# Turning x with VectorE blocks and SBUF-to-SBUF transfers in place of TensorE transposes, under a replanned order

## The chip, the cores and the metric

The kernel runs on one core of one Trainium2 chip. The core has a matrix engine (TensorE, PE in the profile, with its weight loads as PEld), VectorE (DVE), ScalarE (ACT), GpSimd (POOL) and SyncE (SP), each working through a queue of its own in order, and 16 DMA engines. A step on one engine waits for steps on others by semaphores. The metric is the time of one execution on the device in microseconds (us), lower is better.

## What is computed

All in float32. The inputs are q, k, v of shape (8 batches, 8 heads, 576 positions, 64), g_norm (64), and three weights that arrive as float64: w_val and w_out (512 x 512) and conv_w (5 x 512). The reference, cut to what matters:

```python
kv  = einsum('bhsd,bhse->bhde', k, v)
out = einsum('bhsd,bhde->bhse', q, kv)
out = out / sqrt(mean(out * out, axis=-1) + 1e-6) * g_norm
x   = out.transpose(0, 2, 1, 3).reshape(B, S, H * D)        # (8, 576, 512)
gate_pre[:, s] = sum over k of conv_w[k] * xp[:, k + s]     # xp: x with 4 rows of zeros ahead
gate = 1 / (1 + exp(-gate_pre))
result = (gate * (x @ w_val)) @ w_out
```

## The kernel before, in words

Work is cut by batch. For each of the 8 batches there is an attention part and a gated part.

**Attention.** `kv_product` (matmuls at L330) makes the 64 x 64 product of k and v for each head, `kv_copy` (L340) puts pairs of heads on the diagonal of a 128 x 128 tile. q has to be turned so that its 64 features lie on partitions: for batches 0 and 1 by TensorE (`turn_q_rows`, L360, and ScalarE copies that sort the columns), for batches 2 to 7 (`TURNED = 2`) by one VectorE block transpose for each pair of heads (`turn_q`, L348). Then the 576 positions are taken in five chunks, four of 128 and a tail of 64, tail first and the others downwards (`ORDER`). For each chunk: `raw_product` (L399, four matmuls into one of two PSUM banks), `square` on ScalarE (L413), `sums` on VectorE (L421), `powers` on GpSimd (L427, the inverse root), `normalise` on VectorE (L434), which writes the chunk's x as rows of positions, `turn_x` (L445), which turns each 128 x 128 block of x with a TensorE transpose against an identity matrix into PSUM, and `keep_x` on ScalarE (L452), which copies it to SBUF and multiplies by the column gcol (g_norm times 8). What stands in `xT` then is x with features on partitions and positions along the free axis, in the order "t within n", position = t x 18 + n, with n counting 18 blocks of 32 columns. In this order the shift by one position of the convolution is a shift by one block of 32 columns; four extra blocks in front (the halo) are filled by four GpSimd copies (`halo`, L460).

**Gated part.** `gate_start` (L464, ScalarE) makes the first tap of the convolution for one group of 128 features, four `gate_tap` (L470, VectorE, 128 x 576 each) add the others, `gate_end` (L477, ScalarE) applies the sigmoid. `val_product` (L482) is x times w_val, eight products of four matmuls a batch (the profile counts eight matmuls for four of the code, the transposes of x once); `gated` (L491, VectorE) multiplies by the gate. `out_product` (L501) is the product with w_out, 4 or 5 chunks a batch, `keep_out` (L509) copies it out of PSUM, `store` (L516) issues four DMAs of 64 KB on SP's queue.

**Weights** are staged as raw 64-bit words (`stage`, L247) and narrowed to float32 in eight steps a tile, five on VectorE and three on ScalarE (L267 to L293).

**Order.** Nothing is ordered by the loops. Each step is added to a `Planner` with its engine, a modelled duration, a wanted time (`want`), what it needs, gives, takes from a ring of buffers and frees. The planner walks through modelled time: a step can start once its needs are there, a buffer of its ring is free, and not more than `ahead` us before its want (0 for loads); among those that can start first, the one with the earlier want goes. This gives each engine's fixed queue order, which is then emitted. The rings that bear on the change: x rows 3, xT 3, gate 5, qT 2, the raw banks 2, staged weights 3 (4 buffers exist). DMAs are issued by SP alone, except two small loads of g_norm from ScalarE.

Of the kernel before, what the change touches and what calls it, by code (L numbers as in the profile page):

```python
# [15 lines left out]
P = 128  # L16
EPS = 1e-6


class Planner:  # L20


# [5 lines left out]
    HOP = 0.15  # L28
    LANDING = 1.9

    def __init__(self, rings):
        self.rings = {name: {"size": n, "taken": [], "freed": {}} for name, n in rings.items()}
        self.steps, self.done, self.pending = [], {}, []

    def add(self, engine, time, want, fn, *args, needs=(), gives=(), takes=(), frees=(), load=0.0, ahead=12.0):
        self.steps.append(dict(
            engine=engine, time=time, want=want, fn=fn, args=args, needs=list(needs),
            gives=list(gives), takes=list(takes), frees=list(frees), load=load, ahead=ahead, at=len(self.steps)))

    def ready(self, step):  # L40

        t = step["want"] - step["ahead"]
        for key in step["needs"]:
# [4 lines left out]
        for name, _ in step["takes"]:  # L48
# [41 lines left out]
def kernel(  # L90
# [26 lines left out]

    nc = tc.nc  # L120
    B, H, S, D = q.shape
    C = H * D
# [24 lines left out]
    def ps(kind, shape, name):  # L147
        return psum.tile(shape, FP32, tag=kind, bufs=BANKS[kind], name=name)

    plan = Planner({  # L150
# [3 lines left out]
    })  # L154


    tails = [[const.tile([P, H, D], FP32, name=f"{n}l{i}") for n in ("k", "v")] for i in range(2)]
# [84 lines left out]
    def stage(key, src, n, m):  # L242

        size = src.shape[-1]
        t = loads.tile([P, C, 2], U32, tag="w64", bufs=4, name=f"w64_{key[0]}{key[1]}")
        t = t[0:n, 0:m * size, :]
        nc.sync.dma_start(  # L247
            out=t.rearrange("p (m c) w -> p m (c w)", m=m), in_=src.bitcast(U32))
        staged[key] = t

    def narrow(key, dst, n):


        w = staged[key]
        rows, size = w.shape[0], w.shape[1]
        split = lambda a: a if len(dst.shape) == 2 else a.rearrange(
            "p (m c) -> p m c", m=dst.shape[1])
        lo, hi = w[:, :, 0], w[:, :, 1]
        if n == 0:
            staged[key, "parts"] = [  # L260
                work.tile([P, C], kind, tag=tag, bufs=bufs, name=f"{tag}_{key[0]}{key[1]}")[
                    0:rows, 0:size]
                for tag, kind, bufs in (("wexp", U32, 2), ("wman", U32, 1), ("wmf", FP32, 1))]
        e, m, mf = staged[key, "parts"]

        if n == 0:
            nc.vector.tensor_scalar(  # L267
                out=e, in0=hi, scalar1=20, scalar2=0x7FF,
                op0=ALU.logical_shift_right, op1=ALU.bitwise_and,
            )  # L270
        elif n == 1:
            nc.scalar.activation(out=e, in_=e, func=AF.Relu, bias=biases[0:rows, 0:1])
        elif n == 2:
            nc.scalar.activation(out=e, in_=e, func=AF.Relu, bias=biases[0:rows, 1:2], scale=-1.0)
        elif n == 3:
            nc.scalar.activation(
                out=e, in_=e, func=AF.Identity, bias=biases[0:rows, 2:3], scale=-float(1 << 23))
        elif n == 4:
            nc.vector.scalar_tensor_tensor(
                out=e, in0=hi, scalar=0x80000000, in1=e, op0=ALU.bitwise_and, op1=ALU.bitwise_or,  # L280
            )
        elif n == 5:

            nc.vector.tensor_scalar(
                out=m, in0=hi, scalar1=0xFFFFF, scalar2=1 << 20,
                op0=ALU.bitwise_and, op1=ALU.bitwise_or,
            )
        elif n == 6:
            nc.vector.scalar_tensor_tensor(  # L289
                out=mf, in0=lo, scalar=2.0 ** -32, in1=m, op0=ALU.mult, op1=ALU.add,  # L290
            )
        else:
            nc.vector.scalar_tensor_tensor(  # L293
                out=dst, in0=split(mf), scalar=2.0 ** -20, in1=split(e.bitcast(FP32)),
                op0=ALU.mult, op1=ALU.mult,
            )

# [19 lines left out]
    def keep_cw():  # L317

        nc.vector.tensor_scalar_mul(gcol[:], gcol[:], math.sqrt(D))
        nc.vector.tensor_copy(cwT[:], st["cwps"][:])  # L320

    def kv_product(b, hp):
        if hp == 0:
# [21 lines left out]
        return st["qT", b]  # L345

    def turn_q(b, hp):
        nc.vector.transpose(out=new_qT(b)[:, hp, :], in_=st["q", b, hp][:, :, 0:TB])  # L348

    def size(c):  # L350
        return P if c < NJ else T
# [78 lines left out]

    def normalise(b, c):
        n = heads(c)
        x = work.tile([P, C], FP32, tag="x", bufs=3, name=f"x{b}_{c}")
        nc.vector.tensor_tensor(  # L434
            out=x[:, 0:n * D].rearrange("p (h e) -> p h e", h=n),
            in0=st["raw", b, c][:, 0:n * D].rearrange("p (h e) -> p h e", h=n),
# [11 lines left out]
    def keep_x(b, c):  # L448
# [2 lines left out]
        px = st["px", b, c][:].rearrange("p k t -> p (k t)")[:, 0:NK * m]  # L451
        nc.scalar.activation(  # L452
            out=xTs[b % 3][:, :, first:first + m], in_=px.rearrange("p (k t) -> p k t", k=NK),
            func=AF.Copy, scale=gcol[:],
        )

    def halo(b):
        for kc in range(NK):
# [1 line left out]
            nc.gpsimd.tensor_copy(row[:, 0:K - 1, 1:TB], row[:, NB:NB + K - 1, 0:TB - 1])  # L460

    def gate_start(b, jt):
        gate = work.tile([P, S], FP32, tag="gate", bufs=5, name=f"gate{b}_{jt}")
        nc.scalar.activation(  # L464
            out=gate[:], in_=xTs[b % 3][:, jt, HALO:SX], func=AF.Copy, scale=cwT[:, K - 1, jt:jt + 1])
        st["gate", b, jt] = gate
# [62 lines left out]
    def attention(b, first, step, kv_first, turn_first):  # L529

        slow = 1.7 if b == 0 else 1.0
        for hp in range(HP):
# [8 lines left out]
            )  # L541
            if b >= TURNED:
                plan.add(
                    "DVE", 0.77, turn_first + 1.5 * hp, turn_q, b, hp,
                    needs=[("q", b, hp)] + after("qT", b, hp - 1), gives=[("qT", b, hp)],
                    takes=[("qT", b)] if hp == 0 else [], frees=[("q", (b, hp))],
                )
# [23 lines left out]
        for n, c in enumerate(ORDER):  # L571
# [35 lines left out]
            if n == 1:  # L607
                plan.add(
                    "POOL", 1.2, t + 7.0, halo, b, needs=[("xT", b, NJ), ("xT", b, NJ - 1)],
                    gives=[("halo", b)],  # L610
                )

    def gates(b, first, step):
        for jt in range(NK):
# [91 lines left out]
    def weight(key, want, first, step):  # L706
# [5 lines left out]
        for n in range(8):  # L712
# [1 line left out]
            plan.add(  # L714
                "ACT" if n in (1, 2, 3) else "DVE", (0.45, 0.75, 0.75, 0.75, 0.7, 0.45, 0.7, 0.7)[n] * small,
                first + n * step, narrow_weight, *key, n,
                needs=[("staged", key) if n == 0 else ("narrow", key, n - 1)],
                gives=[("narrow", key, n)] + ([key] if n == 7 else []),
                takes=[(ring, key)] if ring else [],
                frees={6: [("w64", key), ("wman", key)], 7: [("wexp", key), ("wmf", key)]}.get(n, []),  # L720
# [67 lines left out]
```

## Time and profile before

| | |
|---|---|
| median of 3 runs | 367.56 us (366.39 to 369.91) |
| profiled execution | 370.04 us |
| its span, first to last instruction | 368.2 us |
| mean granted TensorE clock | 0.979 |
| HBM read, written | 39.21 MB, 9.44 MB |

The profile is of one execution. The span is shorter than the time of the execution by what lies before the first instruction and after the last. "Busy" leaves out DMA issues, semaphores and branches. "Idle before" is the time an engine stood still just ahead of a group, with what ended that wait. The chain is followed back from the last instruction to whatever released it, so its shares add up to the span, while busy times of engines that work side by side do not. Matmuls are pipelined: a single one's duration (275 ns for a transpose of x) overlaps its neighbours', and the chain or a window says better what a group takes.

### The profile page before, as it was taken

Reading aid. Unit: us, or ns where it says so; the run is one execution under the profiler, and the core shown is the slowest. Engines: PE = TensorE matmul, PEld = TensorE weight load, DVE = VectorE, ACT = ScalarE, POOL = GpSimd, SP = SyncE. Lnnn points to the kernel's source line nnn. Section 1 sums busy time; section 2 is a strip of 40 time slices with the busy share of each in tenths; the row PEclk is TensorE's granted clock in tenths of the full one; section 3 lists DMA queues with packets and bytes.
Section 4 is the critical chain, followed back from the end, with each engine's and each line's share of the span. In section 5 each row is a group of like instructions: output and inputs, shape, how many; then the busy total and the mean of one; then the engine's idle time right before and its main releaser. Section 6 shows DMA issues by size and latency. Waiting matters only on the chain.

```text
span 368.2 us, 5537 instructions
## 1 busy us (share of the span) xinstructions
PE 341.9 (93%) x2065; PEld 232.0 (63%) x2065; DVE 215.7 (59%) x363; ACT 142.4 (39%) x253; POOL 73.9 (20%) x82
## 2 busy tenths in 40 slices
PE   4677899869799999999999999999999999999994
PEld 3676687648564786477646785578546874674441
DVE  3075999979932995957329764956239645920000
ACT  3385766715344335422333425313253335201111
POOL 2045025200431153003410241005300450000000
PEclk9989999969899999999999999999999999999998
DMA  7999977922024960595029821981122002201322
GB/s 222 291 291 336 257 204 233 292 61 64 0 53 140 265 194 16 167 274 166 8 65 229 268 84 39 311 239 34 29 57 59 2 0 53 63 2 29 86 75 67
DMA packets 42936, 49.01 MB, mean 133 GB/s; under 512 B 14218, under 2 KB 34718, under 8 KB 42910
## 3 DMA queue, kind: packets, MB, share of 16 engines
q1 hardware_dynamic: 42750, 48.67, 48.0%
q8 instruction: 16, 0.26, 0.3%
q14 instruction: 10, 0.08, 0.1%
q10 hardware_dynamic: 160, 0.00, 0.0%
HBM read 39.21 MB, written 9.44 MB: 132 GB/s over the span
## 4 chain that ended last, share of the span: by engine, by line
PE 83%; SPq 6%; DVE 5%; DMA 3%; ACT 2%; issue 1%; DVEq 0%; ACTq 0%
PE val L482 33%; PE out L501 33%; PE raw L399 8%; PE kv L330 4%; PE xTps L445 4%; DMA v<-in_v_dram 3%; SPq L196 2%; DVE gate L470 2%; SPq L205 2%; SPq L247 1%; PE qTps L360 1%; DVE gv L491 1%; DVE ss L421 0%; DMA out_dram<-ot 0%; DVE wmf_wout L289 0%
## 5 line engine op out<-in xcount | busy, mean ns | idle before, releaser
L482 PE MATMUL val<-xT,wval 128*128 128x288 f32 x512 | 136.4, 414 | 6.9 <-DVE gv L491 6.1
L501 PE MATMUL out<-wout,gv 128*128 128x512 f32 x288 | 127.2, 595 | 0.0
L470 DVE SCALAR_TENSOR_TENSOR gate<-xT,cwT,gate 128x576 f32<-128x576 f32 x128 | 102.8, 816 | 30.2 <-ACT gate L464 27.5
L482 PEld LDWEIGHTS val<-xT,wval 128*128 128x128 f32 x512 | 94.7, 192 | 33.5 <-DVE gv L491 7.2
L427 POOL TENSOR_TENSOR rt<-ss,mhalf 128x8 f32<-128x8 f32 (+1 forms) x40 | 63.5, 1591 | 226.5 <-DVE ss L421 226.5
L501 PEld LDWEIGHTS out<-wout,gv 128*128 128x128 f32 x288 | 53.9, 192 | 61.3 <-issue 61.0
L509 ACT COPY ot<-out 128x512 f32<-128x512 f32 x36 | 21.0, 583 | 82.7 <-PE out L501 53.4
L491 DVE TENSOR_TENSOR gv<-val,gate 128x288 f32<-128x288 f32 x64 | 28.6, 452 | 25.7 <-PE val L482 25.4
L399 PE MATMUL raw<-kvbd,qT 128*128 128x128 f32 (+1 forms) x320 | 41.5, 289 | 1.9 <-ACT kvbd L340 1.9
L399 PEld LDWEIGHTS raw<-kvbd,qT 128*128 128x128 f32 (+1 forms) x320 | 37.6, 191 | 6.9 <-issue 3.4
L452 ACT ACTIVATE xT<-xTps,gcol 128x512 f32<-128x512 f32 (+1 forms) x40 | 25.8, 645 | 39.0 <-PE xTps L445 39.0
L413 ACT ACTIVATE sq<-raw 128x512 f32<-128x512 f32 (+1 forms) x40 | 22.2, 554 | 37.4 <-PE raw L399 37.3
L434 DVE TENSOR_TENSOR x<-raw,rt 128x512 f32<-128x512 f32 (+1 forms) x40 | 25.2, 630 | 19.5 <-POOL rt L427 19.4
L477 ACT ACTIVATE gate<-gate 128x576 f32<-128x576 f32 x32 | 21.8, 682 | 36.2 <-DVE gate L470 36.2
L421 DVE TENSOR_REDUCE ss<-sq 128x8 f32<-128x520 f32 (+1 forms) x40 | 25.3, 634 | 16.3 <-ACT sq L413 16.1
L330 PE MATMUL kv<-v,k 128*64 128x64 f32 x512 | 21.3, 229 | 3.6 <-DMA v<-in_v_dram 3.6
L330 PEld LDWEIGHTS kv<-v,k 128*64 128x64 f32 x512 | 18.4, 142 | 9.8 <-issue 8.6
L445 PE MATMUL xTps<-ident,x 128*128 128x128 f32 x144 | 22.4, 275 | 2.3 <-DVE x L434 2.2
L445 PEld LDWEIGHTS xTps<-ident,x 128*128 128x128 f32 x144 | 17.7, 141 | 10.5 <-issue 6.6
L464 ACT ACTIVATE gate<-xT,cwT 128x576 f32<-128x576 f32 x32 | 22.2, 764 | 0.3
L348 DVE STREAM_TRANSPOSE qT<-q 128x576 f32<-128x576 f32 x24 | 18.1, 766 | 5.4 <-DMA q<-in_q_dram 5.4
L360 PE MATMUL qTps<-ident,q 128*64 128x128 f32 (+1 forms) x160 | 11.6, 308 | 5.1 <-DMA q<-in_q_dram 5.1
(52 smaller groups left out, 99.6 us busy)
## 6 DMA issues: line engine op xcount, KB each, us to landing
q<-in_q_dram SPq DMA_DIRECT2D x96, 140.0 KB, 4.1
out_dram<-ot SPq DMA_DIRECT2D x144, 64.0 KB, 1.7
k<-in_k_dram SPq DMA_DIRECT2D x16, 512.0 KB, 5.4
v<-in_v_dram SPq DMA_DIRECT2D x16, 512.0 KB, 6.6
q<-in_q_dram SPq DMA_DIRECT2D x4, 512.0 KB, 6.4
w_wval<-in_moe_w_val_dram SPq DMA_DIRECT2D x4, 512.0 KB, 8.6
w_wout<-in_moe_w_out_dram SPq DMA_DIRECT2D x4, 512.0 KB, 5.7
kl<-in_k_dram SPq DMA_DIRECT2D x8, 128.0 KB, 6.3
```

The lines of the kernel that those rows point to most:

```text
L330: nc.tensor.matmul(kvp[r * D:(r + 1) * D, hp, :], st["k", b, half][:, h, j, :] if j < NJ else kl[:, 2 * hp + r, :], st["v", b, half][:, h, ...
L399: nc.tensor.matmul(raw[row * m:(row + 1) * m, col * P:(col + 1) * P], st["qT", b][:, hp, c * P:c * P + m], kv_bd[b % 2][:, hp, :], start=T ...
L413: nc.scalar.activation(out=sq[:, 0:n, 0:D], in_=st["raw", b, c][:, 0:n * D].rearrange("p (h e) -> p h e", h=n), func=AF.Square,)
L421: nc.vector.reduce_sum(out=ss[:, 0:n], in_=st["sq", b, c][:, 0:n], axis=AX.X)
L427: nc.gpsimd.tensor_tensor(out=rt[:, 0:n], in0=st["ss", b, c][:, 0:n], in1=mhalf[:, 0:n], op=ALU.pow)
L434: nc.vector.tensor_tensor(out=x[:, 0:n * D].rearrange("p (h e) -> p h e", h=n), in0=st["raw", b, c][:, 0:n * D].rearrange("p (h e) -> p h ...
L445: nc.tensor.transpose(px[:, col, :], st["x", b, c][:, col * P:(col + 1) * P], ident[:])
L452: nc.scalar.activation(out=xTs[b % 3][:, :, first:first + m], in_=px.rearrange("p (k t) -> p k t", k=NK), func=AF.Copy, scale=gcol[:],)
L470: nc.vector.scalar_tensor_tensor(out=gate[:], in0=xTs[b % 3][:, jt, tap * TB:tap * TB + S], scalar=cwT[:, tap, jt:jt + 1], in1=gate[:], op ...
L482: nc.tensor.matmul(val[:], wval[:, kc, jt * P:(jt + 1) * P], xTs[b % 3][:, kc, HALO + n * SV:HALO + (n + 1) * SV], start=(kc == 0), stop=( ...
L491: nc.vector.tensor_tensor(out=gv[:, jt, first:first + SV], in0=st["val", b, jt, n][:], in1=st["gate", b, jt][:, n * SV:(n + 1) * SV], op=A ...
L501: nc.tensor.matmul(po[:], gv[:, jt, c * P:(c + 1) * P], wout[:, jt, :], start=(jt == 0), stop=(jt == NK - 1),)
```

## The change

For batches 2 to 7 the four full chunks of x are no longer turned by TensorE:

- `turn_blocks` (VectorE) transposes the 128 x 512 rows of x in blocks of 32 x 32 into a tile y, one instruction a chunk.
- `move_blocks` (GpSimd queue) then puts the blocks onto their partitions: for each of four groups of columns four DMAs from SBUF to SBUF, each 32 partitions x 4 x 512 bytes (64 KB). All four chunks must be in y before the first group. The groups go from the last columns to the first; the first of them is also given the tail's copy as a need. Per batch that makes 16 transfers.
- So that a block of 32 rows of a chunk is a block of 32 columns of xT, chunk c now holds the blocks n = c, c + 4, c + 8, c + 12 of q: `turn_q` becomes five instructions over the same 576 columns.
- The tail chunk of every batch, and all chunks of batches 0 and 1, still go through `turn_x` and `keep_x`.
- `keep_x` no longer multiplies by gcol. It is multiplied into the taps (`keep_cw`) and into w_val (the last narrowing step), for which that step of w_val now needs cwT.
- Rings: x 3 to 2, gate 5 to 4, staged weights to 3 buffers, y new with 2.
- The planner: `ahead` 12 to 40 us by default; rings tails, kvbd, xT and gv are taken strictly batch by batch; and the table `SHIFTS` is added to the wants, by step and batch (or weight tile).

```diff
+SHIFTS = {
+    "gate_start": {0: 7},
+    "gate_tap": {3: 16.5, 7: 9},
+    "gated": {0: 14.5, 6: -13.5},
+    "halo": {2: -0.5, 4: -69, 6: -5.5},
+    "kv_product": {1: -16, 6: -3},
+    "load_half": {("k", 3): -7, ("k", 4): -27, ("k", 6): -21.5, ("v", 0): -5, ("v", 1): 18, ("v", 2): -5,
+        ("v", 4): -34, ("v", 6): -74},
+    "load_q": {3: 2.5, 4: -1, 5: -3, 6: -5, 7: -12.5},
+    "load_q_rows": {0: -273, 1: 28.5},
+    "load_tails": {0: -53, 3: -20.5, 4: 24},
+    "move_blocks": {3: 35, 7: 5.5},
+    "narrow_weight": {("wout", 1): -14.5, ("wout", 2): -68},
+    "normalise": {2: -16.5},
+    "out_product": {2: -291.5},
+    "powers": {7: -166.5},
+    "raw_product": {0: -10.5},
+    "square": {1: 0.5, 5: -17.5},
+    "stage_weight": {("cw", 0): -385, ("wout", 0): -43, ("wout", 3): -18.5, ("wval", 1): -83.5,
+        ("wval", 2): -40, ("wval", 3): -31.5},
+    "store": {0: -1.5},
+    "sums": {0: -19, 2: -73.5, 4: 6},
+    "turn_q": {3: -15, 5: -59.5},
+    "turn_x": {0: -9.5},
+    "val_product": {0: 15, 1: 47.5, 2: 72, 3: 70.5, 4: 57, 5: 52},
+}
...
-    def add(self, engine, time, want, fn, *args, needs=(), gives=(), takes=(), frees=(), load=0.0, ahead=12.0):
+    def add(self, engine, time, want, fn, *args, needs=(), gives=(), takes=(), frees=(), load=0.0, ahead=40.0):
+        ints = [a for a in args if isinstance(a, int)]
+        which = tuple(a for a in args if isinstance(a, str)) + tuple(ints[:1])
+        want += SHIFTS.get(fn.__name__, {}).get(which[0] if len(which) == 1 else which, 0.0)
...
+            if name in self.by_batch and len(ring["taken"]) != owner:
+                return None
...
+                out=dst, in0=split(mf), scalar=gcol[:] if key[0] == "wval" else 2.0 ** -20, in1=split(e.bitcast(FP32)),
...
-        nc.vector.tensor_copy(cwT[:], st["cwps"][:])
+        nc.vector.tensor_scalar_mul(cwT[:], st["cwps"][:], gcol[:])
+        nc.vector.tensor_scalar_mul(gcol[:], gcol[:], 2.0 ** -20)
...
-        nc.vector.transpose(out=new_qT(b)[:, hp, :], in_=st["q", b, hp][:, :, 0:TB])
+
+        q, qT = st["q", b, hp], new_qT(b)[:, hp, :]
+        for c in range(NJ):
+            nc.vector.transpose(out=qT[:, c * P:(c + 1) * P], in_=q[:, c:NJ * HB:NJ, 0:TB])
+        nc.vector.transpose(out=qT[:, SF:S], in_=q[:, NJ * HB:NB, 0:TB])
...
-            func=AF.Copy, scale=gcol[:],
+            func=AF.Copy,
         )
+
+    def turn_blocks(b, c):
+        if ("y", b) not in st:
+            st["y", b] = work.tile([P, C // TB, NJ, TB], FP32, tag="y", name=f"y{b}")
+        nc.vector.transpose(
+            out=st["y", b][:, :, c, :], in_=st["x", b, c][:].rearrange("p (k i) -> p k i", i=TB))
+
+    def move_blocks(b, a):
+
+        y = st["y", b][:].rearrange("p (k i) c t -> p i k (c t)", i=HB)
+        first = HALO + a * P
+        for i in range(HB):
+            nc.gpsimd.dma_start(
+                out=xTs[b % 3][i * TB:(i + 1) * TB, :, first:first + P],
+                in_=y[a * TB:(a + 1) * TB, i])
...
+            if b >= TURNED and c < NJ:
+                plan.add(
+                    "DVE", 0.75, t + 5.5, turn_blocks, b, c,
+                    needs=[("x", key)] + ([("y", b, ORDER[n - 1])] if n > 1 else []),
+                    gives=[("y", b, c)], takes=[("y", b)] if n == 1 else [], frees=[("x", key)],
+                )
+                continue
...
+        t = first + 4 * step + 6.0
+        if b >= TURNED:
+            for n, a in enumerate(range(HB - 1, -1, -1)):
+                plan.add(
+                    "POOL", 2.4, t + 2.4 * n, move_blocks, b, a,
+                    needs=[("y", b, c) for c in range(NJ)]
+                    + [("xT", b, NJ) if n == 0 else ("moved", b, n - 1)],
+                    gives=[("xT", b, a), ("moved", b, n)], frees=[("y", b)] if a == 0 else [],
+                    load=0.26 / RATE,
+                )
+            t += 3.0
+        plan.add(
+            "POOL", 1.2, t, halo, b, needs=[("xT", b, NJ), ("xT", b, NJ - 1)],
+            gives=[("halo", b)],
+        )
```

More of the change, by code (lines that the diff above doesn't have):

```diff
@@ L244, in stage @@
         size = src.shape[-1]
-        t = loads.tile([P, C, 2], U32, tag="w64", bufs=4, name=f"w64_{key[0]}{key[1]}")
+        t = loads.tile([P, C, 2], U32, tag="w64", bufs=3, name=f"w64_{key[0]}{key[1]}")
         t = t[0:n, 0:m * size, :]
@@ L432, in normalise @@
         n = heads(c)
-        x = work.tile([P, C], FP32, tag="x", bufs=3, name=f"x{b}_{c}")
+        x = work.tile([P, C], FP32, tag="x", bufs=2, name=f"x{b}_{c}")
         nc.vector.tensor_tensor(
@@ L462, in gate_start @@
     def gate_start(b, jt):
-        gate = work.tile([P, S], FP32, tag="gate", bufs=5, name=f"gate{b}_{jt}")
+        gate = work.tile([P, S], FP32, tag="gate", bufs=4, name=f"gate{b}_{jt}")
         nc.scalar.activation(
@@ L716, in weight @@
                 first + n * step, narrow_weight, *key, n,
-                needs=[("staged", key) if n == 0 else ("narrow", key, n - 1)],
+                needs=[("staged", key) if n == 0 else ("narrow", key, n - 1)]
+                + (["cwT"] if n == 7 and key[0] == "wval" else []),
                 gives=[("narrow", key, n)] + ([key] if n == 7 else []),
```

13 lines of the change are left out of this document (5 added, 8 removed), and 4 rows, old and new, of the table plan.

## The prediction, made blind

> **What bounds the kernel now.** I read the page's first part, then one table of windows, then the chain in order of time, then the groups by line. The first part and the windows:
>
> ```profile
> span 368.2 us, 5537 instructions
> PE 341.9 (93%) x2065; PEld 232.0 (63%) x2065; DVE 215.7 (59%) x363; ACT 142.4 (39%) x253; POOL 73.9 (20%) x82
> ...
> 0.00:31.20 31.20, 18.83 (x247) 16.87 (x248) 13.24 (x46) 14.28 (x33) 10.07 (x19) 0.95 1.02 269
> 31.20:100.00 68.80, 59.73 (x507) 47.04 (x508) 59.57 (x101) 39.35 (x72) 14.36 (x12) 0.93 0.65 179
> 100.00:360.00 260.00, 260.00 (x1306) 166.91 (x1305) 142.85 (x218) 87.62 (x147) 49.48 (x52) 1.00 0.38 107
> 360.00:368.20 8.20, 3.31 (x8) 1.14 (x6) 0.00 (x0) 1.13 (x2) 0.00 (x0) 0.87 0.25 64
> ```
>
> The columns of a window are its length, then PE, PEld, DVE, ACT and POOL busy, granted clock, DMA share, GB/s. There are three stages. Up to 31.2 us the DMA engines are full (1.02) and PE waits for data. From 31.2 to 100 PE is idle for 68.80 - 59.73 = 9.1 us and DVE is nearly full. From 100 to 360 PE is busy for 260.00 of 260.00 us: TensorE alone sets the time there, and nothing else can. So whatever leaves PE's queue after 100 us comes off the span in full, as long as PE stays fed. The chain shows what the turning of x costs in that stretch:
>
> ```profile
> 102.70 0.44 PE xTps L445 x4
> ...
> 144.83 0.44 PE xTps L445 x4
> ...
> 306.15 0.44 PE xTps L445 x4
> ```
>
> These are the first, one in the middle and the last of 24 such pieces (four full chunks of each of batches 2 to 7), all 0.44 us, all on the chain.
>
> **What is removed.** The 24 groups of four transposes: 24 x 0.44 = 10.6 us of PE in the full stretch. The 2-transpose group of the 64-row tail stays. The line's own mean (275 ns for one) must not be used: 96 x 0.275 = 26 us counts overlapping matmuls twice. ACT loses 24 copies of L452; it is not a bound (39%), so I count nothing for them.
>
> **What VectorE gains.** Its nearest rows:
>
> ```profile
> L348 DVE STREAM_TRANSPOSE qT<-q 128x576 f32<-128x576 f32 x24 | 18.1, 766 | 5.4 <-DMA q<-in_q_dram 5.4
> L320 DVE COPY cwT<-cwps 128x20 f32<-128x20 f32 x1 | 0.2, 179 | 0.3 <-PE cwps L314 0.3
> L188 DVE MEMSET sq<- 128x8 f32 x2 | 0.1, 65 | 0.0
> ...
> sum 161.32, PE 161.32 PEld 107.94 DVE 105.23 ACT 59.32 POOL 35.06; mean PE 40.33 PEld 26.98 DVE 26.31 ACT 14.83 POOL 8.76
> ```
>
> The last row is the mean over four whole batches (123.86 to 285.18 us): PE 40.33, DVE 26.31, POOL 8.76 us a batch. A block transpose of 512 columns is 512/576 of 766 ns, so 0.68 us (0.77 at most, the whole row): 2.7 us a batch. The transpose of q becomes five instructions over the same 576 columns; the four extra ones cost between 65 and 179 ns each, by the smallest DVE rows: 0.26 to 0.72 us a call, 1.0 to 2.9 us a batch. DVE then has 26.3 + 2.7 + 1.0 to 2.9 (3.1 with the dearer block) = 30.0 to 32.3 us a batch beside a PE that needs 40.33 - 4 x 0.44 = 38.6. Hidden behind PE; if DVE were the bound this would cost 4 to 6 us a batch. The second multiply of gcol is one 128x1 instruction, and gcol as wval's scalar in place of a constant adds none. The shorter ring of x (3 to 2) is filled and emptied by DVE itself, in order; the gate ring of 4 still holds a batch, staging had three in the plan already. Nothing for these; if gate starts did wait they would hold ACT's queue, where the copies that free PE's banks stand.
>
> **What POOL and the DMA engines gain.** Per batch 16 transfers of 64 KB (four groups of four), from SBUF to SBUF, issued by POOL. No row shows a DMA issued by POOL, so I bound it by SP's, and the landing by the stores:
>
> ```profile
> 153.60 2.17 SPq L516 DMA_DIRECT2D out_dram<-ot  x4
> ...
> 60.59 0.60 SPq L205 DMA_DIRECT2D kl<-in_k_dram  x1
> ...
> 18.31 2.11 SPq L205 DMA_DIRECT2D vl<-in_v_dram  x1
> ...
> out_dram<-ot SPq DMA_DIRECT2D x144, 64.0 KB, 1.7
> q1 hardware_dynamic: 42750, 48.67, 48.0%
> 167.97 1.01 POOL L427 TENSOR_TENSOR rt<-ss,mhalf 128x4 f32<-128x4 f32 x1 [25.42 <-DVE ss L421]
> ```
>
> Issue costs between 0.54 us (2.17/4, a store of the same 64 KB over 32 partitions) and 2.11 us (an issue into a full queue in the loading stage). I take 0.60, nearest in shape and away from the loading stage: 9.6 us a batch. POOL then has 8.76 + 9.6 = 18.4 of 38.6 us, and the last row shows where it fits: POOL sits idle for 25.4 us between two batches' powers. The first group waits for all four blocks; behind it in POOL's queue stand its sisters, the halo copy and the next batch's powers, for which VectorE's normalise waits, and behind that the two raw banks of PE. With 9.6 us inside a gap of 25 that wait costs nothing; without the gap it costs what is late. Data: a packet now takes 0.48 x 16 x 368.2 / 42750 = 66 ns of one engine; 24 x 4 x 128 = 12288 new rows of 512 B, at that price, are 51 us of sixteen engines, and lift the share in the long stretch from 0.38 to some 0.57. Queue SP gets none of them.
>
> The Trainium skill speaks against this edit: "DMA: Bandwidth & Descriptors", section "Anatomy of one DMA", gives a DMA issued by GpSimd a fixed cost of about 2.0 us. If POOL were held that long, it would need 8.76 + 32 = 40.8 us a batch by an estimate from that page, over PE's 38.6, and the sum would be 353.0 + 6 x 2.2 = 366. The same section puts most of the 2 us into the wait for the receipt, which need not hold POOL; no run here shows it yet.
>
> **What the new order moves.** Staging of wval and wout and batch 0's tails and q get earlier wants than k and v of batch 0; `ahead` goes from 12 to 40 us, products of batches 0 to 5 are wanted 15 to 72 us later, so that attention of later batches is taken first whenever it is ready. In the long stretch order gains nothing (PE is full). The early stage can win or lose:
>
> ```profile
> 70.91 0.79 ACT gate L464
> 71.72 0.83 DVE gate L470
> ...
> 76.60 0.46 DVE gv L491
> 77.11 4.21 PE val L482 x8
> 81.31 2.01 PE kv L330 x40
> 83.32 2.15 PE val L482 x8
> ...
> 88.65 0.61 DVE wmf_wout L289
> 89.28 0.69 DVE wout L293
> ...
> 95.13 0.69 DVE wmf_wout L289
> ```
>
> At 70 to 77 us PE waits for the gates of batch 1 though batch 2's kv (81.31) could fill the hole, and the product behind it takes 4.21 instead of 2.15 us; at 88 to 96 the narrowing of wout stands on the chain between gates. DVE was idle for 31.20 - 13.24 = 18 us in the loading stage. Upper end: all 9.1 us of idle and the 2.1 us of the slow product come back, 11.2. Lower end: one weight tile of 0.52 MB ahead of k and v delays the start by 0.52 MB / 269 GB/s = 1.9 us, and batch 2's four blocks and four split transposes (4 x 0.77 + 4 x 0.72 = 6.0 us less what hides) land in the full DVE, of which I count 4.5: together -6.4. I take +4.0, above the middle, because both the narrowing and the filler work are free to come earlier.
>
> **Sum.** 10.6 + 4.0 = 14.6 us. The profiled execution took 370.04 us (span 368.2 and 1.8 around it), so it becomes 355.4; it lay 2.5 us above the median of the runs, 367.56, which becomes **353.0 us**.
>
> **The rivals.**
>
> *The early stage loses.* The reordering costs the 6.4 us above instead of winning 4. For: DVE is the busiest there (59.57 of 68.80) and gets more. Against: the holes are order, not work. 367.56 - 10.6 + 6.4 = 363.4 us.
>
> *x comes too late.* The distance from x to the product that reads it, batch 3:
>
> ```profile
> 142.72 0.65 DVE L434 TENSOR_TENSOR x<-raw,rt 128x512 f32<-128x512 f32 x1
> 145.35 0.69 ACT L452 ACTIVATE xT<-xTps,gcol 128x512 f32<-128x512 f32 x1
> 155.40 2.10 PE L482 MATMUL val<-xT,wval 128*128 128x288 f32 x8
> ```
>
> Now the turned x stands 2.7 us after the last normalise (146.04 - 143.37) and 9.4 us before the product. The new way takes 0.68 + 16 x 0.60 + 1.7 = 12.0 us, 9.3 us more: at the old distance it fits by a hair. Each 0.1 us more per transfer would cost 1.6 us a batch, 9.6 in six. At 0.75 us, with the distance unchanged, PE stands 2.3 us in each batch, 14 in all: 353.0 + 14 = 367 us, the gain gone. Against: `ahead` and the later wants lengthen that distance.
>
> *POOL becomes the bound* (the other side). PE's 38.6 us leave (38.6 - 8.76)/16 = 1.86 us a transfer; beyond that POOL paces every batch, whatever the order. At 2.11 us, SP's dear row, POOL needs 42.5 us, 3.9 more than PE, and six batches make 353.0 + 23.5 = 376.5 us. For: no DMA from POOL is in the trace, and SP's issues into a full queue do cost that. Against: in the long stretch the engines are 0.38 busy, and SP issues its stores there at 0.54. (With the page's 2.0 us this would be the case, at its 366.)
>
> That PE doesn't lose the transposes I give nothing: the planner adds them only for tails and batches 0 and 1.
>
> **How the numbers follow.** Forecast 0.55, early loss 0.17, late x 0.12, POOL the bound 0.16. The first two are faster by over 1% (about what a measurement of this kernel can tell from no change): 0.72; late x is within 1%: 0.12; slower 0.16. The low end is all early idle regained, 367.56 - 10.6 - 11.2 = 345.8, rounded down to 345; the high end takes in late x, 368, and leaves out POOL's case. The likeliest case alone spans 346 to 360.
>
> **What would show it.** Right: 2065 - 96 = 1969 matmuls; PE full from about 100 us to the end; POOL's idle time before its powers shrunk, but normalise waiting for powers little longer than now; VectorE near 240 us; a span near 353.6 with PE near 331 us busy. Wrong: idle PE before products or raw products after 100 us, released by transfers (late x) or by normalise behind a late power (POOL); more than 9.1 us idle in the stretch before 100 us (early loss); transfers issued at over 1.8 us.

## The result, and the profile after

The changed kernel takes **353.47 us** (median of 4 runs, 352.09 to 354.26); beside it on the same chip the kernel before took 367.44 (median of 4). The ratio, of the mean times, is 0.961 (95% interval 0.955 to 0.967): 14.5 us less by the means, 14.0 by the medians. The forecast was 353.0. The profiled execution took 352.09 us, with a span of 350.3.

The first part of its page and its table of windows, in the columns of the one shown of before (length, PE, PEld, DVE, ACT, POOL busy, granted clock, DMA share, GB/s):

```profile
span 350.3 us, 5671 instructions
PE 327.5 (93%) x1969; PEld 221.6 (63%) x1969; DVE 235.6 (67%) x484; ACT 124.5 (36%) x229; POOL 128.0 (37%) x178
```

```profile
0.00:31.20 31.20, 17.62 (x223) 16.00 (x223) 14.54 (x49) 16.42 (x37) 5.55 (x13) 0.89 1.00 289
31.20:100.00 68.80, 65.45 (x548) 48.51 (x549) 64.48 (x129) 38.54 (x76) 24.36 (x21) 0.98 0.76 212
100.00:340.00 240.00, 239.16 (x1189) 155.04 (x1188) 156.55 (x308) 68.34 (x117) 98.09 (x145) 1.00 0.50 129
340.00:350.30 10.30, 5.29 (x13) 2.07 (x11) 0.00 (x0) 1.17 (x2) 0.00 (x0) 1.00 0.29 75
```

Length less PE busy is PE's idle time, stage by stage: loading 13.6 us (12.4 before), 31 to 100 us 3.4 (9.1 before), the long stretch 0.84 (0 before), the tail 5.0 (4.9 before). So idle time fell by 3.5 us, and busy time by 341.9 - 327.5 = 14.4: together the 17.9 us by which the two spans differ. The transposes of x are 10.6 of the 14.4. The other 3.8 go with a clock of 0.98 in place of 0.93 between 31 and 100 us and 1.00 in place of 0.87 in the tail, while in loading it fell from 0.95 to 0.89; I can't divide them further. The profiled execution of before lay 2.6 us above its median and that of the changed kernel 1.4 below, which is why the spans differ by more than the medians.

PE is still the bound. From 266 us its chain has three unbroken pieces. In the kernel before, raw products and transposes of x still stood between such pieces, the last of them at 306; with the new wants all attention is done ahead of them:

```profile
266.18 17.17 PE out L559 x40
283.35 31.04 PE val L540 x128
314.39 27.48 PE out L559 x64
```

What the new work costs, by the page's groups and its DMA part:

```profile
q0 software_dynamic: 3072, 6.30, 7.7%
...
L511 POOL DMA_DIRECT2D xT<-y x96 | 52.8, 556 | 17.0 <-DVE y L503 10.7
...
L477 DVE TENSOR_TENSOR x<-raw,rt 128x512 f32<-128x512 f32 (+1 forms) x40 | 25.2, 629 | 5.9 <-POOL rt L470 5.1
...
L390 DVE STREAM_TRANSPOSE qT<-q 128x128 f32<-128x128 f32 x96 | 20.7, 274 | 0.2 <-DMA q<-in_q_dram 0.2
...
L503 DVE STREAM_TRANSPOSE y<-x 128x512 f32<-128x512 f32 x24 | 16.9, 706 | 0.6
...
xT<-y POOLq DMA_DIRECT2D x96, 64.0 KB, 2.8
```

POOL is held 556 ns per transfer, the data lands 2.8 us after issue (median), and VectorE's normalise waits 5.1 us in all for POOL's powers (19.4 in the kernel before). One place shows how little room there is. In the chain around the only stall of the long stretch, batch 3's transfer is what the gate waits for, and behind the gate's taps on VectorE stands the normalise that PE needs:

```profile
144.79 1.04 POOL rt L470
145.83 0.86 POOL xT L511 x2
146.69 0.25 issue
146.94 0.54 POOL xT L511
147.48 7.27 DMA xT<-y
...
154.85 0.79 ACT gate L522
...
165.38 0.61 DVE x L477
...
166.03 1.16 PE raw L442 x8
```

### The profile page after: what moved, and what is told of

Same layout as the page of the kernel before. It is cut to its first block, busy times and chain, and to the rows that moved or that the text cites. A ratio compares the mean times of both kernels' runs of the same rounds, so it can differ in the third digit from the quotient of the medians.

```text
span 350.3 us, 5671 instructions
## 1 busy us (share of the span) xinstructions
PE 327.5 (93%) x1969; PEld 221.6 (63%) x1969; DVE 235.6 (67%) x484; ACT 124.5 (36%) x229; POOL 128.0 (37%) x178
## 3 DMA queue, kind: packets, MB, share of 16 engines
q0 software_dynamic: 3072, 6.30, 7.7%
## 4 chain that ended last, share of the span: by engine, by line
PE 78%; DVE 8%; DMA 7%; ACT 3%; POOL 2%; issue 1%; SPq 1%; DVEq 0%; ACTq 0%; POOLq 0%
PE val L540 33%; PE out L559 30%; PE raw L442 7%; DVE gate L528 4%; PE kv L369 4%; DMA w_wval<-in_moe_w_val_dram 2%; DMA xT<-y 2%; DMA q<-in_q_dram 2%; POOL rt L470 1%; PE xTps L488 1%; PE qTps L403 1%; DVE qT L390 1%; DVE ss L464 1%; DVE x L477 1%; ACT gate L522 0%
## 5 line engine op out<-in xcount | busy, mean ns | idle before, releaser
L540 PE MATMUL val<-xT,wval 128*128 128x288 f32 x512 | 129.7, 408 | 0.0
L559 PE MATMUL out<-wout,gv 128*128 128x512 f32 x288 | 125.4, 592 | 0.0
L511 POOL DMA_DIRECT2D xT<-y x96 | 52.8, 556 | 17.0 <-DVE y L503 10.7
L442 PE MATMUL raw<-kvbd,qT 128*128 128x128 f32 (+1 forms) x320 | 38.9, 279 | 3.3 <-DVE x L477 2.4
L442 PEld LDWEIGHTS raw<-kvbd,qT 128*128 128x128 f32 (+1 forms) x320 | 35.2, 180 | 10.0 <-issue 3.9
L549 DVE TENSOR_TENSOR gv<-val,gate 128x288 f32<-128x288 f32 x64 | 28.3, 453 | 16.0 <-PE val L540 14.6
L369 PE MATMUL kv<-v,k 128*64 128x64 f32 x512 | 22.3, 238 | 5.6 <-DMA k<-in_k_dram 5.6
L369 PEld LDWEIGHTS kv<-v,k 128*64 128x64 f32 x512 | 19.8, 151 | 9.6 <-issue 8.6
L390 DVE STREAM_TRANSPOSE qT<-q 128x128 f32<-128x128 f32 x96 | 20.7, 274 | 0.2 <-DMA q<-in_q_dram 0.2
L503 DVE STREAM_TRANSPOSE y<-x 128x512 f32<-128x512 f32 x24 | 16.9, 706 | 0.6
L403 PEld LDWEIGHTS qTps<-ident,q 128*64 128x64 f32 (+1 forms) x160 | 10.8, 171 | 6.9 <-POOL vl L218 4.3
```

What stands on the lines that cost most here:

```text
L369: nc.tensor.matmul(kvp[r * D:(r + 1) * D, hp, :], st["k", b, half][:, h, j, :] if j < NJ else kl[:, 2 * hp + r, :], st["v", b, half][:, h, ...
L390: nc.vector.transpose(out=qT[:, c * P:(c + 1) * P], in_=q[:, c:NJ * HB:NJ, 0:TB])
L403: nc.tensor.matmul(pq[r * D:(r + 1) * D, hp, 0:m], st["q", b, half][:, h, j, :] if j < NJ else st["q", b, 2][:, 2 * hp + r, :], ident[0:m, ...
L442: nc.tensor.matmul(raw[row * m:(row + 1) * m, col * P:(col + 1) * P], st["qT", b][:, hp, c * P:c * P + m], kv_bd[b % 2][:, hp, :], start=T ...
L511: nc.gpsimd.dma_start(out=xTs[b % 3][i * TB:(i + 1) * TB, :, first:first + P], in_=y[a * TB:(a + 1) * TB, i])
L540: nc.tensor.matmul(val[:], wval[:, kc, jt * P:(jt + 1) * P], xTs[b % 3][:, kc, HALO + n * SV:HALO + (n + 1) * SV], start=(kc == 0), stop=( ...
```

## The experiments

The theory going in was the forecast's: 10.6 us are PE's transposes, 4 us the early stage, and the long stretch gains nothing from its order since PE is full there. The rival: the new way needs the table, because x comes later.

### The transposes put back, unread

```diff
+        px = ps("tp", [P, NK, P], f"again{b}_{a}")
+        flat = st["y", b][:].rearrange("p k c t -> p (k c t)")
+        for col in range(NK):
+            nc.tensor.transpose(px[:, col, :], flat[:, col * P:(col + 1) * P], ident[:])
         for i in range(HB):
             nc.gpsimd.dma_start(
```

> The new kernel with 24 groups of four TensorE transposes put back as extra work: at each group of moves PE also transposes four 128 x 128 pieces of y into a PSUM tile that nobody reads; the result doesn't depend on them. Theory (the gain is PE time taken out of a full queue): 24 x 0.44 = 10.6 us come back, 353.5 + 10.6 = 364 us. Rival (most of the gain comes from the new order, PE's queue has slack): under 357 us.

Measured: 363.88 us (363.28 to 364.76), ratio 0.988 (0.984 to 0.992). Against the changed kernel's ratio, (0.9880 - 0.9606) x 367.4 = 10.1 us come back, by the two intervals some 2.6 us more or less: the term of 10.6. And with the same matmuls as before, the kernel is still 1.2% faster, 4.4 us (3.0 to 5.8): that is everything but the transposes, where I had put 4.0. Its window says where the matmuls went:

```profile
100.00:340.00 240.00, 239.84 (x1261) 160.93 (x1260) 157.73 (x311) 66.92 (x114) 98.78 (x145) 1.00 0.49 126
```

PE is as full as without them, with 72 more matmuls in the window; the work just runs on for longer.

### The kernel before with three of four transposes left out

```diff
-        for col in range(heads(c) * D // P):
+        for col in range(1 if b >= TURNED and c < NJ else heads(c) * D // P):
...
+        if b >= TURNED and c < NJ:
+            nc.scalar.activation(
+                out=xTs[b % 3][:, :, first:first + m],
+                in_=st["px", b, c][:, 0:1, :].broadcast_to((P, NK, P)), func=AF.Copy, scale=gcol[:],
+            )
+            return
```

> The kernel before, three of the four transposes left out for the full chunks of batches 2 to 7, the copy out of PSUM taking the one block four times (x is not computed rightly); order, DVE, POOL and DMAs as before. Theory: 24 x 3 x 0.11 = 7.9 us less, 367.4 - 7.9 = 359.5 us. Rival (the transposes were hidden in the pipelined queue): 366 to 367 us.

Measured: 361.28 us (360.62 to 365.31), ratio 0.983 (0.977 to 0.989): 6.3 us (3.9 to 8.6) for the 7.9 expected; one of the four runs, at 365.31, makes the interval wide. The same term from the other side: under the old order, with none of the new work, PE's transposes are worth their time on the chain.

### The new way under the old wants

```diff
-SHIFTS = {
...
-}
+SHIFTS = {}
...
-    def add(self, engine, time, want, fn, *args, needs=(), gives=(), takes=(), frees=(), load=0.0, ahead=40.0):
+    def add(self, engine, time, want, fn, *args, needs=(), gives=(), takes=(), frees=(), load=0.0, ahead=12.0):
```

> The new kernel with an empty table of shifts and the lookahead back at 12 us, so nearly the old wants; turning by blocks and moves stays. Theory (order is worth only the early stage's 4 us): 357 us, PE still full after 100 us. Rival (x comes too late at the old distance: 0.7 + 16 x 0.55 + 2.8 of landing = 12.3 us where there were 2.7, against a slack of 9.4): PE stands still ahead of products in each batch, 362 us or more.

The planner lays the queues out anew in this run, from the old wants and its modelled times of the new steps, so this isn't the order of before but what the old wants make of the new path.

Measured: 408.78 us (407.08 to 409.4), ratio 1.109 (1.104 to 1.114). The theory fell here. The rival, which asked for 362 or more, holds, but far beyond its own price: against the changed kernel's ratio the table (with `ahead`) is worth (1.109 - 0.961) x 367.4 = 54 us, not 4. With the table empty and `ahead` left at 40:

> The new kernel with an empty table of shifts, lookahead kept at 40 us. Theory: the long stretch stays full, the early stage loses what the shifts of loads and weights gave, 357 us. Rival (the table is what gives x its distance): 362 us or more; with both this and the run with 12 us at 357 the distance never mattered.

Measured: 418.18 us (415.68 to 419.88), ratio 1.136 (1.128 to 1.143). So `ahead` by itself doesn't help; without the table it costs another 10 us. Below are the waits of PE over the whole execution (line, line waited for, total us, times, longest) and the windows of the first of the two, the one with `ahead` at 12. Its lines are numbered 25 lower than the changed kernel's, since the table is gone (L515 is the product, L524 the multiplication by the gate):

```profile
PE val L515 <- DVE gv L524: 28.9, 11, 7.8
PE val L515 <- DMA xT<-y: 8.2, 1, 8.2
PE raw L417 <- DVE x L452: 5.4, 5, 1.8
```

```profile
100.00:340.00 240.00, 207.15 (x1066) 134.79 (x1065) 143.71 (x289) 60.64 (x105) 95.82 (x135) 0.94 0.49 128
...
sum 408.00, PE 342.61 PEld 229.49 DVE 235.46 ACT 124.91 POOL 126.61; mean PE 85.65 PEld 57.37 DVE 58.87 ACT 31.23 POOL 31.65
```

In the long stretch PE stands 32.9 us idle: 17.6 of it before products whose bank of PSUM is freed only when a gate is done (the rest of the 28.9 falls outside), 8.2 before one product that waits for a transfer, and 5.4 before raw products that wait for normalise. That isn't the whole loss: the same 1969 matmuls keep PE busy 342.6 us instead of 327.5, at a granted clock of 0.94 instead of 1.00. Of the 55.0 us between the two spans (405.3 and 350.3), 15.1 are slower matmuls and 39.9 are idle time.

### The old turning in the new kernel, without the table

```diff
-            if b >= TURNED and c < NJ:
+            if False:
...
-        t = first + 4 * step + 6.0
-        if b >= TURNED:
+        t = first + step + 7.0
+        if False:
```

The transpose of q is the single one of before as well; the table is empty and `ahead` is 12, everything else is new.

> x and q turned as before the change (TensorE, ScalarE copies), with everything else of the new kernel: batch-strict rings, the smaller rings of x and gates, gcol in the weights, no table, lookahead 12 us. Theory (what costs 55 us with the old wants is the new path's latency alone): 366 to 370 us, the time before. Rival (the smaller rings or the strict batch order cost it): 390 us or more.

Measured: 367.18 us (365.57 to 369.3), ratio 0.999 (0.996 to 1.003). So with the old turning the shorter rings, the strict order of batches and the moved gcol cost nothing. The (1.109 - 0.999) x 367.4 = 40 us between this kernel and the one above are those of the new path (blocks, transfers, the split transposes of q) and of the order that the planner makes for it, under wants that were laid out for the old one. And of the 4.4 us that the first experiment found besides the transposes nothing is left here, with neither the table (and its `ahead`) nor the new path. That they are the table's is the likely reading, not a shown one: the old turning was not run with the table.

### Is it the length of the transfers?

Without the table, only the first of the four transfers of each group is made (the rest of xT holds ones), which takes 12 issues and most of the data out of the path; and the same edit with the table.

```diff
-        for i in range(HB):
+        for i in range(1):
             nc.gpsimd.dma_start(
```

> The run with the old wants (empty table, lookahead 12 us: 408.8 us, x 13 to 35 us from its last block to the first gate), of each group of four transfers only the first is issued; the other 96 partitions of x hold a constant set once at the start (x is not computed rightly). All waits from blocks to transfers to gates stay, DVE's and PE's work and every order too. Theory (the length of that path is what costs 55 us): the path falls to 5 to 10 us and most of the loss comes back, 360 to 372 us. Rival (the wants themselves, or DVE's added blocks and split transposes, cost it): over 395 us.

> The new kernel with its table, again with only the first transfer of each group (x is not computed rightly). Theory (with the table the transfers cost nothing, PE is full without them as with them): 351 to 354 us. Rival (the transfers still cost some us a batch in powers held back or in traffic): under 350 us.

Measured without the table: 401.99 us (401.89 to 404.95), ratio 1.097 (1.092 to 1.102). Against the same kernel with all transfers that is 1.2% of 367.4, some 4 us (2.5 more or less, by the two intervals). So most of the loss isn't time that the engines spend waiting for transfers: in this trace one gate start of the last six batches still waits for one, 1.80 us. The fixed orders, which the planner laid out for transfers of full length, stayed as they were, so this run doesn't rule out the length that was planned for. Measured with the table: 352.89 us (351.48 to 353.41), ratio 0.961 (0.957 to 0.964), which is the changed kernel's own. With the table the transfers cost nothing that can be measured: PE reads 240.00 of 240.00 us in the long stretch with a quarter of them and 239.16 with all.

### Is it POOL's queue?

All 16 transfers of a batch stand where its first group stood, so no power of the next batch can get between them; table empty, `ahead` 12.

```diff
+        if a < HB - 1:
+            return
+        for a in range(HB - 1, -1, -1):
```

> The run with the old wants (408.8 us), with one change in POOL's queue: all 16 transfers of a batch are issued where the first group stood, so that no group stands behind a power of the next batch. Every other queue has the same order. With the old wants a last group waited there for up to 19 us (y of batch 4 done at 193.4, its last group issued at 212.97, behind a power whose sums came late). Theory (POOL's queue, not the transfers' own time, makes x late): 370 to 392 us. Rival (the orders of PE, DVE and ACT, made for late x, cost it whatever POOL does): 398 us or more.

Measured: 405.14 us (403.5 to 405.83), ratio 1.104 (1.099 to 1.110): some 2 us back, less than the intervals can tell from nothing. POOL's queue isn't what costs either, as far as this move changes it. But with the transfers in one place the trace can be read through. The timelines of POOL, ACT and PE (start, length, the work, the idle time ahead of it and what ended it), for batch 4 (L489 are the transfers, L500 the gate's start, L518 the product, L537 the out product):

```profile
190.51 8.71 POOL L489 DMA_DIRECT2D xT<-y  x16 [2.38 <-issue]
199.21 0.97 POOL L496 COPY xT<-xT 128x124 f32<-128x124 f32 x4
```

```profile
205.34 0.59 ACT L545 COPY ot<-out 128x512 f32<-128x512 f32 x1 [2.85 <-PE out L537]
205.89 0.38 ACT L431 ACTIVATE sq<-raw 128x256 f32<-128x256 f32 x1
206.97 0.60 ACT L431 ACTIVATE sq<-raw 128x512 f32<-128x512 f32 x1 [0.69 <-PE raw L417]
213.07 0.39 ACT L470 ACTIVATE xT<-xTps 128x256 f32<-128x256 f32 x1 [5.50 <-PE xTps L463]
213.90 0.60 ACT L431 ACTIVATE sq<-raw 128x512 f32<-128x512 f32 x1 [0.45 <-PE raw L417]
214.80 0.60 ACT L431 ACTIVATE sq<-raw 128x512 f32<-128x512 f32 x1 [0.30 <-PE raw L417]
217.29 0.75 ACT L354 COPY kvbd<-kv 64x256 f32<-64x256 f32 x2 [1.89 <-PE kv L344]
218.06 2.77 ACT L500 ACTIVATE gate<-xT,cwT 128x576 f32<-128x576 f32 x4
```

```profile
187.93 17.33 PE L537 MATMUL out<-wout,gv 128*128 128x512 f32 x40
...
227.07 3.85 PE L518 MATMUL val<-xT,wval 128*128 128x288 f32 x8 [6.93 <-DVE gv L527]
231.47 2.21 PE L518 MATMUL val<-xT,wval 128*128 128x288 f32 x8 [0.55 <-DVE gv L527]
```

The last transfer is issued at 199.2 and the halo done at 200.2, yet the gate starts at 218.06. ScalarE is mostly idle until then, but works in order: ahead of the gate in its queue stand squares of the next batch, a tail's copy and a copy of kv, each waiting for PE, and PE was in 17.33 us of out products until 205.3. At 220 PE then runs out of work and stands 6.93 us for the gates that it had itself held up. So here it is the place of the gate's start in ScalarE's fixed queue that costs, not a transfer. The other batches of the new path agree: none of their gate starts waits for a transfer in this trace, and they come 3.6 to 16.9 us after the issue of the last one has ended (18.8 in batch 4). This also leaves little for the rival that the two runs hide each other's gain, since with the groups together no transfer is waited for at a gate's start at all.

### Can the wants be mended by one move?

The products later and nothing else of the table (`ahead` 40); and attention 30 us earlier, with the loads that are laid out from it, and no table (`ahead` 40).

```diff
+SHIFTS = {"val_product": {0: 15, 1: 47.5, 2: 72, 3: 70.5, 4: 57, 5: 52}}
```

```diff
-            first = begin - (28.0 if b == 1 else 34.0)
+            first = begin - (28.0 if b == 1 else 64.0)
```

> The new kernel with one row left of the table: the products of batches 0 to 5 wanted 15 to 72 us later, lookahead 40 us (418 us without any row). Theory (the rows that put attention ahead of products are what makes room for the transfers): half or more of the 65 us come back, 370 to 390 us. Rival (the table works only as a whole, or by its other rows): 400 us or more.

> The new kernel with an empty table and a lookahead of 40 us, as in the run without shifts (418 us), with one number changed: attention of batches 3 to 7 is wanted 64 us ahead of its products' end instead of 34. Theory (with the old wants the blocks of a batch follow the gates of the batch before on DVE, so that the transfers run while DVE has nothing to do; distance is what the table gives): half of the loss comes back, 385 to 400 us. Rival (transfers, smaller rings or POOL's queue cost the time, wherever they stand): stays at 410 to 420 us.

Measured: with the products later 381.84 us (380.69 to 384.05), ratio 1.041 (1.035 to 1.047). Against the empty table, 418.18, that one row gives (1.136 - 1.041) x 367.4 = 35 us back (some 3.4 more or less) of the 64 that the table is worth there (1.136 - 0.961). Attention 30 us earlier took 408.7 us (408.33 to 413.92), ratio 1.115 (1.107 to 1.124), between what the two theories asked for: 0.021 x 367.4 = 8 us back. That settles only that this bare distance of 30 us isn't what the table gives.

### How much room the table leaves

Each transfer split in two, and in four, the same bytes, table as it is:

```diff
-            nc.gpsimd.dma_start(
-                out=xTs[b % 3][i * TB:(i + 1) * TB, :, first:first + P],
-                in_=y[a * TB:(a + 1) * TB, i])
+            for k in range(0, NK, 2):
+                nc.gpsimd.dma_start(
+                    out=xTs[b % 3][i * TB:(i + 1) * TB, k:k + 2, first:first + P],
+                    in_=y[a * TB:(a + 1) * TB, i, k:k + 2])
```

> The new kernel, each of the 96 transfers split in two by feature groups: 32 transfers a batch instead of 16, the same bytes, rows and order. POOL then needs 8.9 + 32 x 0.55 = 26.5 us a batch, under PE's 38.6, and x lands some 9 us later. Theory A (the table leaves x a distance well over 9 us): 353 to 356 us. Theory B (x is there only just in time): a stall of up to 9 us in each batch, 365 us or more.

> The same with each transfer split in four: 64 a batch. POOL needs 8.9 + 64 x 0.55 = 44 us a batch, 5.5 over PE's 38.6. The bound of 1.86 us a transfer (for 16) that the prediction worked out says: POOL paces, at least 353.5 + 6 x 5.5 = 386 us, more where its lateness also holds powers and so DVE. If issue is not what counts (a split transfer costs POOL a quarter each): 353 to 357 us.

Measured: in two 372.48 us (369.92 to 375.02), ratio 1.016 (1.009 to 1.022); in four 466.21 us (465.29 to 467.14), ratio 1.269 (1.262 to 1.275). Groups of the page for the split in two:

```profile
L512 POOL DMA_DIRECT2D xT<-y x192 | 101.9, 538 | 23.0 <-DVE y L503 12.7
...
L477 DVE TENSOR_TENSOR x<-raw,rt 128x512 f32<-128x512 f32 (+1 forms) x40 | 25.2, 631 | 29.2 <-POOL rt L470 28.4
...
L523 ACT ACTIVATE gate<-xT,cwT 128x576 f32<-128x576 f32 x32 | 23.0, 767 | 31.8 <-DMA xT<-y 29.5
```

An issue of half the size still takes 0.54 us, so twice as many cost (101.9 - 52.8) / 6 = 8.2 us of POOL more in each batch. POOL's own load, 8.8 + 17.0 = 25.8 us a batch, is far from PE's 38.6; yet normalise now waits 28.4 us for powers queued behind transfers (5.1 in the changed kernel), and the gates 29.5 us for transfers. The time goes up by 0.055 x 367.4 = 20 us, as theory B had it (365 or more), though in shorter stalls than the 9 us that it named. Between 100 and 340 us PE now stands 14.6 us idle (0.8 in the changed kernel), in waits of at most 2.85 us, the largest parts before raw products that wait for normalise (6.2) and before products that wait for gates (4.2). For the split in four, the mean load of POOL would be 8.8 + 64 x 0.50 = 40.8 us a batch, 2.2 over PE's need and 13 in six batches; it lost 113.

## Why the prediction was right, and where it was not

**PE's transposes: right.** 10.6 us forecast, 10.1 by putting them back, 6.3 for 7.9 by leaving out three quarters of them. The 1969 matmuls and the near-full PE from 100 us to the end are as it said; PE busy was put at 331 and is 327.5.

**The early stage: right in size.** +4.0 forecast, 4.4 (3.0 to 5.8) measured as all that isn't transposes. The windows place it: idle time between 31 and 100 us fell by 5.7, and loading lost 1.2, the direction in which the weights' earlier loads were to push it. The size within its range of -6.4 to +11.2 was a choice, and that it came this close is in part luck. The step was that PE's holes are order and can be filled. In the chain of the changed kernel PE stands alone from 60 to 100 us, and where a product came late after the gates of batch 1 there is now other work of PE and the product at its usual length:

```profile
59.84 4.37 PE val L540 x18
...
71.92 1.94 PE val L540 x8
73.87 1.31 PE kv L369 x40
75.18 2.14 PE val L540 x8
...
99.34 0.73 PE val L540 x3
```

**POOL's issue: right, a little dear.** 0.60 us forecast, 0.556 measured (9.6 and 8.9 us a batch). The page "DMA: Bandwidth & Descriptors" of the Trainium skill, section "Anatomy of one DMA", gives a DMA from GpSimd 2.0 us fixed and puts most of it in the wait for the receipt. The trace agrees in so far as the 2.0 us don't hold POOL: it is held 0.55, and the landing comes later (whether the receipt makes up the rest, no run here shows):

```profile
L511 POOL DMA_DIRECT2D xT<-y x96: 548/548/725, 103.4 to 282.7; - x96
...
DMA to landing us min/median/max: 1.9/2.8/7.3
```

The landing I had taken from the stores at 1.7; it is 1.9 at least, 2.8 in the middle and 7.3 at worst. POOL as the bound did not come, since 0.556 is far under the 1.86 that would have made it so.

**VectorE: right.** The blocks take 706 ns (0.68 to 0.77 forecast). q's five pieces take (20.7 + 4.9) / 24 = 1.07 us in place of 0.766, 0.30 more a call, near the low end of 0.26 to 0.72; the 4.9 is the group of the 64-column pieces:

```profile
L391 DVE STREAM_TRANSPOSE qT<-q 128x64 f32<-128x64 f32 x24 | 4.9, 204 | 0.0
```

VectorE is 235.6 us busy, near the 240 named, and hidden.

**DMA engines: too dear, and harmless.** I priced 12288 rows at 66 ns, 51 us of sixteen engines. They went as 3072 packets, four rows in each, and took 7.7% of the span, 27 us; the share of the long stretch is 0.50, not 0.57.

**The order in the long stretch: wrong.** The step that failed is "In the long stretch order gains nothing (PE is full)", and with it, under *x comes too late*, "at the old distance it fits by a hair". PE was full in the kernel before, where x needs 2.7 us to be turned. I carried that fullness over to a kernel in which it needs 12, and asked of the old order only whether 12 fits ahead of the product. But the product isn't the first reader of x. In batch 3 of the kernel before, the gate's start reads it 0.03 us after the last copy (which ends at 146.04), and VectorE stands 3.51 us for that start:

```profile
146.07 2.78 ACT L464 ACTIVATE gate<-xT,cwT 128x576 f32<-128x576 f32 x4
146.88 11.55 DVE L470 SCALAR_TENSOR_TENSOR gate<-xT,cwT,gate 128x576 f32<-128x576 f32 x14 [3.51 <-ACT gate L464]
```

So the 9.4 us of slack were those of the product; the gate's start followed x at once, and what x is late moves the taps, 11.55 us of VectorE in this row, by as much. The gates had a slack of their own (the first was done at 150.98, its first use came at 158.35), which the prediction didn't look at. How much of the loss comes by this way was not measured. That 12 doesn't fit, the runs show: under the old wants the new way takes 408.8 us, the old turning 367.2; the new way with the table 353.5. The table isn't a small extra of 4 us beside the change; without it the change loses 40 us against before. The forecast came out right because the table is part of the change and does what I took for granted (I gave late x a chance of 0.12). To that extent the number was luck: nothing in the working could tell whether the table gives x enough room.

The rival's price was wrong too, by the same reasoning. It counted what was late in a batch, 2.3 us, and called it 14 in six. The loss without the table has two parts that it left out. One is queue order: taking out three quarters of the transfers gives back 4 us and moving them on POOL's queue 2, while the trace shows the gate's start held behind the next batch's steps on ScalarE, which is read from it and was not tested. The other is the clock: of the 55 us, 15.1 are the same matmuls running slower. That the later wants of the products alone bring back about half of the table's worth, 35 of 64 us, is shown; which of its other rows carry the rest, and whether moving the gate's start alone would, stays open.

**POOL in the way of the powers: right in kind, wrong in point.** I let it decide at 1.86 us a transfer, where POOL's load passes PE's. Two issues of 0.54 us in place of one cost 20 us, at 1.08 us for what was one transfer and with POOL idle a third of the time that PE needs for a batch. Here a queue that alternates between two urgent kinds of work was late long before it was full.

No run was clearly faster than the changed kernel: what PE has left to lose is 13.6 us in loading, 3.4 before 100 us, 0.8 after and 5.0 in the tail.

## What to carry to other kernels

Taking work off the engine that bounds a stage is worth its time on the chain, and can be priced from the groups there; but when a step is moved to a path that takes longer, "the engine is full" holds only for the order that filled it, so price the new path under the old order as well, and ask for each step behind it what it stands behind in its own queue. An engine with spare time on average still delays what is queued behind a burst on it: look at the longest run of its new work against the slack of the next urgent step, not at the load. And ask of the path not only when its last reader needs the data, but when the first one does. Long stalls of TensorE cost more than themselves: 17.2 us of idle time in the long stretch, in four stalls of up to 9.2, went with a granted clock of 0.96 there (the run with the products later), 14.6 us in stalls of at most 2.85 with 0.99 (the split in two).

## What the hardware showed that was not expected

**A long stall slows the matmuls after it.** In the kernel with the groups together, the product behind the 6.93 us of waiting took 3.85 us, the next 2.21. Two windows there, with the granted clock third from the end:

```profile
226.00:231.00 5.00, 3.85 (x8) 2.52 (x8) 3.42 (x6) 1.31 (x2) 0.00 (x0) 0.56 0.08 27
231.00:234.00 3.00, 2.53 (x20) 1.83 (x22) 2.93 (x5) 0.00 (x0) 0.00 (x0) 1.00 0.00 0
```

0.56, then 1.00. The Trainium skill's "TensorE: Matmul & The Clock Gate", Part 1, states that the clock falls to half after an idle window of some 3.4 us and comes back after about as long a busy one; the trace agrees, with 0.56 over 3.85 us of matmuls behind 6.93 us of idle time. The prediction's own fence had it as well: 4.21 us for a product behind a wait of PE (5.01 us), 2.15 for the next. The length of the stall matters: in the run without shifts the products behind stalls of 5.8 to 8.0 us took 4.21 us each, the one behind 3.44 us the usual 2.21.

**POOL's issue time hardly depends on the size**: 0.556 us for 64 KB, 0.538 for 32 KB, 0.499 for 16 KB, each one transfer from SBUF to SBUF. The 64 KB transfers went as 3072 packets of four rows of 512 bytes, the 32 KB ones as 6144 of two, the 16 KB ones as 12288 of one.
